# A softmax attention and feed-forward kernel whose on-chip tiles get new start addresses

## The chip, the cores and the metric

The kernel runs on one core of one Trainium2 chip. The metric is the device time of one execution in microseconds; below, a time of the kernel is the median of several runs.

## What is computed

All tensors are float32. The reference, cut to what matters:

```python
S, D, F, H, Dh = 2048, 512, 1792, 32, 16
xn = layernorm(x)                                # over D, eps 1e-5
q, k, v = split_heads(xn @ wqkv)                 # 32 heads of 16
s = merge_heads(softmax(q @ k.T * Dh ** -0.5) @ v) @ wo
h = maximum(xn @ w1 + b1, 0) ** 2                # the squared ReLU
out = x + s * silu(h @ w2 + b2)
```

## The kernel before

Everything runs in one program whose order of instructions is written out by hand (`tc.manual_schedule()`); the tile framework adds only the waits between engines. `fast_path` does all the work. `general_path` follows it in a branch that is not taken here.

**Precision.** Most products take float32 operands split in a rounded high part (type float32r, suffix `h` in tile names) and a rest (suffix `l`), and add three products: high with high, high with low, low with high. Values and row sums use plain float32.

**Stage one**, some 150 us. Four chunks of 512 rows are normalised and transposed into `xT` (tiles KA0 and KA1 for chunks 0 and 2, and xh0, xh1, xl0, xl1 for chunks 1 and 3). `linear` (line 117) makes the values: for each block of 128 rows, 12 products of 128 rows by 128 columns against 512 columns of the weights, which lie split in wf1h0, P8, wf1l0 and P9. Queries and keys are made by a Strassen-Winograd scheme from products of half blocks: `product` (line 305) adds six products of 128 x 128 against 512. Its weights (the stationary side) lie in wf2, hh, hl, or, as sums, in KA2, P6 and P7 and other P tiles; its right sides (the moving side) in KA0 and KA1, xh and xl, or, for sums, in u, y, P14, P15, V0, V1. The results go to DRAM and come back later, permuted.

**Stage two**, 64 turns of about 16.5 us. A turn covers 8 blocks of 128 keys for four heads and 512 queries. For each block, `score` (line 494) makes four products on half the rows, two at a time on rows 0 to 63 and 64 to 127: the weights are 128 keys of KA0, KA1 or KA2 (which take turns, in this order, with every load of 1,024 keys), the right side is QA0 or QA1. ScalarE takes the exponentials (line 498) into the tiles P0 to P15, a pair for each of eight blocks; VectorE copies a part of the scores out first (line 517). Between the score products, in an order given by a string of letters, stand products of the feed-forward layers (line 542), also on half the rows in pairs: `first` (weights wf1h0 and wf1l0, right sides xh and xl) and `second` (weights hh and hl, right sides wf2h and wf2l). In the middle of a turn `swap` changes the banks of the two halves, with a memset of one element on GpSimd as a fence (line 568). At the end of the turn the values of the eight blocks follow as one row (line 841): 64 records of TensorE, four heads on four groups of 32 columns, with weights from V0 or V1 (16 key blocks of 83 words each, `NK` and `QW` in the code) and right sides from P.

**The last turns** multiply by the output weights and add the gate and x.

**Addresses.** A tile is named by its tag. The pool `keep` lies first in a partition, then the pool `sb`. In each pool a tag gets its place at its first request, behind the tags that were asked for before, its size rounded up to 32 bytes a partition; later tiles of the tag use the same place. `keep` begins 128 bytes behind a multiple of 512, with `ident` (512 bytes a partition), `nvalid` (4) and `stat` (320). In `sb` the order is that of the code's first use: `ou0`, `b1t`, `eps`, `b2b`, `note`, `P4`, `KA2`, `P5`, `QA0`, `QA1` and so on, with tiles of a few bytes (`st0`, `rs0`, `mv0`, `okm`) among the large ones.

```python
return (p or ps.get(tag, sb)).tile(shape, dt, tag=tag, name=f"{tag}_{cnt[0]}")
```

Of the kernel before, what the change touches and what calls it, by code (L numbers as in the profile page):

```python
# [24 lines left out]
FT = mybir.dt.float32  # L25
FR = mybir.dt.float32r
I32 = mybir.dt.int32
# [11 lines left out]
NK = S // 128  # L39
VW = 560  # L40
QW = 83
# [6 lines left out]
@with_exitstack  # L48
def mha_ffn_kernel(ctx: ExitStack, tc: tile.TileContext, x, wqkv, wo, bx, w1, b1, w2, b2, out):
    nc = tc.nc  # L50
    x, out = x[0], out[0]
    ctx.enter_context(tc.manual_schedule())
    keep = ctx.enter_context(tc.tile_pool(name="keep", bufs=1))
    dram = ctx.enter_context(tc.tile_pool(name="dram", bufs=1, space=DRAM))

    ident = keep.tile([128, 128], FT, name="ident")
    make_identity(nc, ident)
    nvalid = keep.tile([1, 1], I32, name="nvalid")
    stat = keep.tile([128, 80], FT, name="stat")

    kdram = [[dram.tile([128, 2, 1024], FT, name=f"kd{g}_{h}") for h in range(2)] for g in range(4)]
    qdram = [[dram.tile([128, 2, 512], FT, name=f"qd{g}_{c}") for c in range(NC)] for g in range(4)]
    vdram = dram.tile([NK, 128, VW], FT, name="vd")
    xdram = [dram.tile([128, 2, 4, 512], FT, name=f"xd{c}") for c in range(3)]
    sdram = {(a, p): dram.tile([128, 2, 4, 2, 128], FT, name=f"sd{a}{p}") for a in "kq" for p in range(2)}

    udram = [[dram.tile([2, 2, 16, 4, 512], FT, name=f"ud{g}_{c}") for c in range(NC)] for g in range(4)]
    zdram = [[dram.tile([4, 512], FT, name=f"zd{q}_{c}") for c in range(NC)] for q in range(NQ)]
    gdram = dram.tile([S, D], FT, name="gd")

    with tc.tile_pool(name="sb", bufs=1) as sb, ExitStack() as banks:
        fast_path(tc, sb, banks, locals())
    general_path(tc, dram, nvalid, ident, vdram, kdram, qdram, gdram, x, wo, out)


def fast_path(tc, sb, banks, env):
    nc = tc.nc
    ident, nvalid, stat = (env[n] for n in ("ident", "nvalid", "stat"))
    kdram, qdram, vdram, xdram, sdram, udram, zdram, gdram = (
        env[n] for n in ("kdram", "qdram", "vdram", "xdram", "sdram", "udram", "zdram", "gdram"))  # L80
    x, wqkv, wo, w1, b1, w2, b2, out = (
# [9 lines left out]
    def t(shape, dt, tag):  # L91

        cnt[0] += 1
        if tag in BUFS:
            turn[tag] = turn.get(tag, -1) + 1
            n = turn[tag] % BUFS[tag]
            p, tag = ps.get(tag), f"{tag}{places[n] if tag == 'S' else n}"
        else:
            p = None
        return (p or ps.get(tag, sb)).tile(shape, dt, tag=tag, name=f"{tag}_{cnt[0]}")  # L100

    def cast(eng, dst, src):
        if eng is act:
            act.copy(dst, src)
        else:
            eng.tensor_copy(dst, src)  # L106
# [16 lines left out]


    b1raw = t([14, 128], FT, "ou0")
    b1t = t([128, 14], FT, "b1t")
    eps = t([128, 1], FT, "eps")
    dve.memset(eps, EPS)
    b2b = t([128, D], FT, "b2b")

# [423 lines left out]
    note, notes = t([1, 128], FT, "note"), [0]  # L554
# [264 lines left out]
    tags = (("P2", "gl", "P1"), ("P3", "P6", "P7"), ("wf2h0", "wf2l0", "wf2h1"), ("wf2l1", "gl", "KA2"))  # L819
# [196 lines left out]
    for j, c in enumerate(ORDER):  # L1016
        for i in range(2):
            n = per * (j + 1) + i - 1 if j < 3 else LAST + 2 + i
# [85 lines left out]
    for n in range(TURNS):  # L1104
        i = 8 * n
# [68 lines left out]
    ok, okm, ones = t([128, 80], FT, "ok"), t([128, 1], FT, "okm"), t([128, 1], FT, "ones")  # L1174
# [162 lines left out]
```

## Time and profile before

| | |
|---|---|
| Time, median of 3 runs | 1218.28 us (1217.95 to 1218.51) |
| Time of the profiled execution | 1218.33 us |
| Its span, first to last instruction | 1216.6 us |
| Mean granted clock of TensorE | 0.998 |
| TensorE products, busy | 1205.6 us, 99%, 9877 instructions |
| ScalarE, busy | 1042.8 us, 86% |
| VectorE, busy | 846.7 us, 70% |
| GpSimd, busy | 350.4 us, 29% |

How to read the profile's lines. PE is TensorE (PEld its weight loads), ACT is ScalarE, DVE is VectorE, POOL is GpSimd; L117 is line 117 of the kernel. A line of the page's first part gives busy time, share of the span and number of instructions of each engine; the chain of work that ended last tells whose work filled the span. A line of the waits reads: who waited, for whom, us in total, how often, the longest. A line of the timeline gives the start in us, the length in us, engine, line and operation, tile written and tiles read, then the sizes and the number of instructions that follow one another (x2); the end of a product is modelled, and products overlap, so the rate of products is read from the distance of the starts. A line of the table by stretches gives the stretch, its length and the busy time (with the number of instructions) of the engines, then the granted clock, the busy share of the DMA engines and the GB/s; where it is asked for one line of the kernel, only TensorE's products and weight loads appear.

### The profile page before, as it was taken

What the parts mean: (1) busy time and instruction counts of PE and PEld (TensorE: products, weight loads), DVE (VectorE), ACT (ScalarE), POOL (GpSimd) and SP (SyncE); (2) the same over time, 40 slices, a digit from 0 to 9 for tenths busy, and PEclk for the clock granted to TensorE, in tenths of its full rate; (3) what the DMA queues carried; (4) which work ended last, traced back from release to release, by engine and by line L of the source; (5) the groups of instructions that cost most, each with busy time, mean ns of one, the idle gap of its engine ahead of it and who ended that gap; (6) DMA issues with size and microseconds to landing.
All of it is one profiled execution on the core that took longest, in us unless ns stands there. A gap on an engine that the chain in (4) does not pass through costs nothing.

```text
span 1216.6 us, 24228 instructions
## 1 busy us (share of the span) xinstructions
PE 1205.6 (99%) x9877; PEld 714.0 (59%) x9877; DVE 846.7 (70%) x1365; ACT 1042.8 (86%) x1231; POOL 350.4 (29%) x268
## 2 busy tenths in 40 slices
PE   9999999999999999999999999999999999999996
PEld 8888755555555555555555555555555555655553
DVE  7666777576767776757677666667775758777776
ACT  6645589899889889888999888889898889999983
POOL 5756523040312320304032122221230403222222
PEclk9999999999999999999999999999999999999999
DMA  7799915131353223224423133151422232465544
GB/s 289 279 357 317 358 58 136 42 112 45 96 153 91 83 65 81 79 79 148 119 75 99 60 89 93 45 169 48 126 79 80 77 99 80 131 198 159 156 136 106
DMA packets 107576, 154.91 MB, mean 127 GB/s; under 512 B 43386, under 2 KB 57736, under 8 KB 107460
## 3 DMA queue, kind: packets, MB, share of 16 engines
q1 hardware_dynamic: 104804, 144.93, 37.7%
q0 software_dynamic: 2368, 7.87, 2.2%
q8 instruction: 78, 1.28, 0.4%
q10 hardware_dynamic: 288, 0.52, 0.1%
q14 instruction: 38, 0.31, 0.1%
HBM read 103.61 MB, written 49.67 MB: 126 GB/s over the span
## 4 chain that ended last, share of the span: by engine, by line
PE 96%; DVE 1%; POOL 1%; DMA 1%; issue 0%; SPq 0%; ACT 0%; DVEq 0%; POOLq 0%
PE acc L841 36%; PE S L542 28%; PE S L494 14%; PE acc L494 5%; PE B L305 5%; PE B L117 3%; PE lin L494 2%; PE D L305 1%; PE B L672 1%; DMA hl<-gd 1%; PE D L243 0%; PE S L984 0%; PE lin L305 0%; PE acc L305 0%; SPq L871 0%
## 5 line engine op out<-in xcount | busy, mean ns | idle before, releaser
L498 ACT ACTIVATE P<-S 128x1024 f32<-128x1024 f32 x702 | 662.8, 1035 | 94.3 <-PE S L494 92.4
L841 PE MATMUL acc<-P,V 128*32 128x512 f32 x4096 | 453.6, 594 | 0.0
L517 DVE COPY P<-acc 128x512 f32<-128x512 f32 x322 | 222.6, 691 | 140.0 <-PE lin L494 67.3
L498 ACT ACTIVATE P<-P 128x1024 f32<-128x1024 f32 x322 | 314.5, 1082 | 0.0
L841 PEld LDWEIGHTS acc<-P,V 128*32 128x32 f32 x4096 | 126.1, 110 | 287.0 <-issue 265.5
L494 PE MATMUL S<-QA,KA 64*128 64x512 f32 x1404 | 291.7, 403 | 0.0
L517 DVE COPY P<-lin 128x512 f32<-128x512 f32 x322 | 220.4, 684 | 2.7 <-PE lin L494 0.6
L494 PEld LDWEIGHTS S<-QA,KA 64*128 64x128 f32 x1404 | 135.3, 184 | 108.2 <-issue 41.8
L494 PE MATMUL lin<-QA,KA 64*128 64x512 f32 x322 | 127.6, 396 | 0.0
L494 PE MATMUL acc<-QA,KA 64*128 64x512 f32 x322 | 127.1, 395 | 0.0
L110 POOL TENSOR_TENSOR wf1l<-wr,wf1h 128x1024 fp32r<-128x1024 f32 x28 | 68.5, 2446 | 176.6 <-DVE wf1h L106 108.3
L568 POOL MEMSET note<- 1x1 f32 x68 | 6.0, 88 | 385.2 <-PE S L542 383.7
L542 PE MATMUL S<-xl,wf1h 64*128 64x512 f32 x464 | 96.5, 390 | 0.0
L110 POOL TENSOR_TENSOR hl<-T,hh 128x1024 fp32r<-128x1024 f32 x28 | 80.1, 2861 | 52.9 <-DVE hh L106 52.9
L110 POOL TENSOR_TENSOR wf2l<-wr,wf2h 128x1024 fp32r<-128x1024 f32 x28 | 67.7, 2417 | 90.3 <-DVE wf2h L106 90.3
L542 PE MATMUL S<-xh,wf1l 64*128 64x512 f32 x480 | 91.7, 391 | 0.0
L542 PE MATMUL S<-wf2l,hh 64*128 64x512 f32 x448 | 91.3, 390 | 0.0
L867 DVE TENSOR_TENSOR ou<-acc,ou 128x512 f32<-128x512 f32 x31 | 21.4, 692 | 96.6 <-PE acc L841 86.8
L542 PE MATMUL S<-wf2h,hl 64*128 64x512 f32 x448 | 83.8, 390 | 0.0
L542 PE MATMUL S<-xh,wf1h 64*128 64x512 f32 x480 | 77.9, 392 | 0.0
L542 PE MATMUL S<-wf2h,hh 64*128 64x512 f32 x448 | 72.3, 394 | 0.0
L494 PEld LDWEIGHTS acc<-QA,KA 64*128 64x128 f32 x322 | 59.3, 184 | 16.5 <-DVE P L517 2.4
(370 smaller groups left out, 1432.2 us busy)
## 6 DMA issues: line engine op xcount, KB each, us to landing
wr<-in_B_w_dram SPq DMA_DIRECT2D x56, 512.0 KB
QA<-qd SPq DMA_DIRECT2D x128, 128.0 KB
KA<-kd SPq DMA_DIRECT2D x64, 256.0 KB
u<-ud SPq DMA_DIRECT2D x15, 512.0 KB
kd<-P SPq DMA_DIRECT2D x11, 512.0 KB
V<-vd SPq DMA_DIRECT2D x8, 664.0 KB
qd<-P SPq DMA_DIRECT2D x9, 512.0 KB
vd<-P SPq DMA_DIRECT2D x16, 280.0 KB
```

Of the source, the lines that this page charges most:

```text
L110: leng.tensor_tensor(lo, src, hi.bitcast(FT), op=OP.subtract)
L117: mm(dst, lhs(a, k), rhs(b, k), start=n == 0, stop=n == len(todo) - 1)
L305: mm(dst, left[a][:, k], right[b][:, k], start=n == 0, stop=n == 5)
L494: mm(dst, k[r, p, 128 * (kb % 8):128 * (kb % 8) + 128], q[r, p], start=True, stop=True)
L498: act.activation(ptile[i, p], src, AF.Exp, scale=SCALE)
L517: dve.tensor_copy(ptile[i, p][:, hp], sides[hp])
L542: ins = mm(bank, self.lhs(a, k)[r], self.rhs(b, k)[r], start=n == 0 and self.at[other] == 0, stop=n == len(self.todo[half]) - 1 and self.a ...
L568: f = pool.memset(note[:, notes[0]:notes[0] + 1], 0.0)
L672: mm(idle[:, :128], ident, ident, start=True, stop=True)
L841: mm(sides[0][32 * j:32 * j + 32], vq[qd][:, kb, 17 * j:17 * j + 32], ptile[i, j // 2][:, j % 2], start=first, stop=last)
L867: dve.tensor_tensor(ou, sides[0], part[0], op=OP.add)
```

## The change

No instruction is added, taken away or moved. In `keep`, the three small tiles (`eps` is now one of them) are asked for ahead of `ident`. At the head of `fast_path`, every large tag of `sb` is asked for once, at its full size, in a new order: the sixteen P tiles, the KA tiles, the QA and split tiles, the others of the same size, then the smaller ones, and between V0 and V1 (5,312 bytes each) small tiles that fill up to the next multiple of 512. These first tiles are never read or written; they only fix the places. `ident` and all large tiles then begin at a multiple of 512 bytes. The slices that TensorE reads inside a tile begin 512 bytes apart or a multiple of it, but for those of V, which begin 332 bytes apart from key block to key block and 68 from head to head, as before.

```diff
+    nvalid = keep.tile([1, 1], I32, name="nvalid")
+    stat = keep.tile([128, 80], FT, name="stat")
+    eps = keep.tile([128, 1], FT, name="eps")
     ident = keep.tile([128, 128], FT, name="ident")
     make_identity(nc, ident)
-    nvalid = keep.tile([1, 1], I32, name="nvalid")
-    stat = keep.tile([128, 80], FT, name="stat")
...
+    split_tiles = [f"{a}{n}" for a in ("xh", "xl", "wf2h", "wf2l", "hh", "hl") for n in range(2)]
+    for tags, n in (((f"P{i}" for i in range(16)), 1024), (("KA0", "KA1", "KA2"), 2048),
+                    (("QA0", "QA1", "wf1h0", "wf1l0", *split_tiles), 1024),
+                    (("T0", "T1", "wr0", "wr1", "gl", "u0", "u1", "y0", "y1"), 1024), (("ou0", "ou1", "b2b"), 512),
+                    (("note",), 128), (("V0",), NK * QW), (("st0", "st1"), 12), (("rs0", "rs1", "mv0", "mv1"), 8),
+                    (("okm", "warm"), 1), (("V1",), NK * QW)):
+        for tag in tags:
+            sb.tile([128, n], FT, tag=tag, name=f"{tag}_first")
...
-    eps = t([128, 1], FT, "eps")
     dve.memset(eps, EPS)
```

More of the change, by code (lines that the diff above doesn't have):

```diff
@@ L77, in fast_path @@
     nc = tc.nc
-    ident, nvalid, stat = (env[n] for n in ("ident", "nvalid", "stat"))
+    ident, nvalid, stat, eps = (env[n] for n in ("ident", "nvalid", "stat", "eps"))
     kdram, qdram, vdram, xdram, sdram, udram, zdram, gdram = (
```

## The prediction

> **What bounds the kernel now.** I read the page first, then the waits, then the order of TensorE's own instructions.
>
> ```profile
> span 1216.6 us, 24228 instructions
> PE 1205.6 (99%) x9877; PEld 714.0 (59%) x9877; DVE 846.7 (70%) x1365; ACT 1042.8 (86%) x1231; POOL 350.4 (29%) x268
> ...
> PE 96%; DVE 1%; POOL 1%; DMA 1%; issue 0%; SPq 0%; ACT 0%; DVEq 0%; POOLq 0%
> ```
>
> The span is 1216.6 us and the profiled execution took 1218.33 us, so 1.7 us lie around the span; the median of the runs is 1218.28. Sums below go against 1218.3. TensorE is busy for 99% and makes 96% of the chain that ended last. A layout changes no instruction, so it must change the time of TensorE's steps, or of what TensorE waits for.
>
> ```profile
> ACT P L498 <- PE S L494: 92.4, 73, 2.4
> ...
> PEld S L494 <- ACT P L498: 18.6, 88, 0.8
> ```
>
> In the view of waits ScalarE waits 92.4 us for TensorE's scores. TensorE's weight loads wait 18.6 us for ScalarE, part of it under running products. So a TensorE that is some 10 us faster finds the room it needs, and one that is slower puts the whole loss on the span.
>
> **The rate of products against the start addresses.** The pool lays its tags in the order in which they are first asked for, each rounded up to 32 bytes, so the starts of the kernel before, taken modulo 512 bytes, come out as these: KA0, KA1, wf1h0, wf1l0, P8, P9 at 352; KA2, QA0, QA1, P4 to P7, P10 to P12 at 64; wf2, hh, hl, V0, T1 at 32; x, u, y, P0 to P3, P13 to P15 at 224. Slices of a tile (V's apart) start 512 bytes or a multiple of that further on, so a product keeps the remainders of its two tiles. The same product of line 117, with the same right sides (wf1, P8, P9 at 352), runs twice:
>
> ```profile
> 62.29 0.63 PE L117 MATMUL B<-P,KA 128*128 128x512 f32 x2
> 62.76 0.62 PE L117 MATMUL B<-wf1l,KA 128*128 128x512 f32 x2
> 63.22 0.62 PE L117 MATMUL B<-P,KA 128*128 128x512 f32 x2
> 63.67 0.61 PE L117 MATMUL B<-wf1h,KA 128*128 128x512 f32 x2
> ...
> 72.75 0.62 PE L305 MATMUL D<-xh,KA 128*128 128x512 f32 x2
> ```
>
> ```profile
> 99.78 0.62 PE L117 MATMUL B<-wf1h,xh 128*128 128x512 f32 x2
> ...
> 110.94 0.40 PE L305 MATMUL D<-xh,KA 128*128 128x512 f32 x1
> ```
>
> With weights from KA0 and KA1 (352, the remainder of the right side) the 40 products from 63.67 to 72.75 us take 9.08 us, 227 ns each; the pieces of two start every 0.45 or 0.46 us throughout. With weights from xh and xl (224 against 352) the 48 products from 99.78 to 110.94 take 11.16 us, 232.5 ns each. The run with equal remainders does not start at its rate: the pieces at 62.29 and 62.76 are 0.47 and 0.46 us before the next, about 233 ns a product, and only then does it settle.
>
> ```profile
> 62.00:73.00 11.00, 11.00 (x50) 9.05 (x50) 5.91 (x13) 5.55 (x9) 6.20 (x4) 1.00 0.99 314
> 99.50:111.00 11.50, 11.50 (x51) 9.31 (x51) 10.15 (x15) 6.43 (x13) 5.74 (x5) 1.00 0.85 296
> ```
>
> The faster stretch has the busier DMA (0.99 against 0.85) and the same clock (1.00), so neither makes the difference. VectorE is less busy in it (5.91 of 11.00 us against 10.15 of 11.50), which a third and a fourth row weigh:
>
> ```profile
> 47.46 1.57 PE L305 MATMUL B<-u,KA 128*128 128x512 f32 x6
> 48.87 1.57 PE L305 MATMUL B<-y,KA 128*128 128x512 f32 x6
> ```
>
> ```profile
> 22.55 0.62 PE L305 MATMUL B<-KA,wf2l 128*128 128x512 f32 x2
> 23.00 1.08 PE L305 MATMUL B<-KA,wf2h 128*128 128x512 f32 x4
> 23.92 0.62 PE L305 MATMUL B<-KA,wf2l 128*128 128x512 f32 x2
> 24.38 1.08 PE L305 MATMUL B<-KA,wf2h 128*128 128x512 f32 x4
> 25.29 0.62 PE L305 MATMUL B<-KA,wf2l 128*128 128x512 f32 x2
> 25.75 1.18 PE L305 MATMUL B<-KA,wf2h 128*128 128x512 f32 x4
> ```
>
> ```profile
> 46.00:51.70 5.70, 5.70 (x26) 4.55 (x26) 2.79 (x13) 2.42 (x6) 5.70 (x6) 1.00 0.30 112
> 22.00:27.50 5.50, 5.50 (x26) 4.32 (x25) 5.34 (x15) 4.36 (x7) 3.82 (x4) 1.00 1.04 403
> ```
>
> Weights from KA2 (64) against u (224): six products in 1.41 us, 235 ns each, with VectorE at 2.79 of 5.70 us and DMA at 0.30. Weights from wf2 (32) against KA0 (352): 14 products in 3.20 us, 228.6 ns, with VectorE at 5.34 of 5.50 and DMA at 1.04. So the step follows the two addresses and not the company: 227 ns for equal remainders, 228.6 for 32 against 352, 232.5 for 224 against 352, 235 for 64 against 224. Each pairing repeats whenever it comes back.
>
> [...]
>
> **The change, part by part.**
>
> *Stage one* (up to 150 us, products over all 128 rows):
>
> ```profile
> 0.00:150.00 150.00, 45.87 (x192) 35.51 (x192) 1.00 0.90 324
> ```
>
> ```profile
> 0.00:150.00 150.00, 80.87 (x336) 62.40 (x336) 1.00 0.90 324
> ```
>
> ```profile
> 40.40 0.70 PE L117 MATMUL B<-wf1h,xh 128*128 128x512 f32 x2 [0.18 <-ACT y L337]
> ```
>
> The rows are line 117 (192 products) and line 305 (336). By the code, half of the 192 (chunks 0 and 2, weights from KA) are of the 227 ns kind and the other 96 of the 232.5 kind; of the 336, the 16 products of six with KA on the right, 96, are of the 228.6 kind, and the other 240 near 235. After the change all pairings are 0 against 0. If they run as 352 against 352 do: 96 x 5.5 + 96 x 1.6 + 240 x 8 ns = 2.6 us. A quarter of these products lies ahead of 40.40 us, where TensorE waits for ScalarE and VectorE's chain anyway, so I take 2.0 us; bounds 0 and 2.6.
>
> *The scores and the feed-forward products* (lines 494 and 542) run as pairs on the two halves of the rows, 40 pairs in a turn (16 of scores, 24 of the other), 64 turns:
>
> ```profile
> 150.00:1200.00 1050.00, 434.18 (x2012) 225.81 (x2012) 1.00 0.33 99
> 150.00:1200.00 1050.00, 502.01 (x2988) 321.66 (x2988) 1.00 0.33 99
> ```
>
> ```profile
> 621.00 0.62 PE L542 MATMUL S<-xh,wf1h 64*128 64x512 f32 x4
> ...
> 629.81 0.40 PE L494 MATMUL S<-QA,KA 64*128 64x512 f32 x2
> ```
>
> 5,000 products (2012 of line 494 and 2988 of 542) are 2,500 pairs; in the turn shown the 38 steps from 621.00 to 629.81 take 8.81 us, 232 ns a pair. Here scores (KA at 352 or 64 against QA at 64) alternate with feed-forward pairs (352 against 224, or 32 against 32), so no long row of equal remainders ever occurs, and what it would do is not in the trace. The lower bound is the settled 227 ns: 5 ns x 38 x 64 = 12.2 us. The other bound is no gain. What the trace has on partly equal turns:
>
> ```profile
> 266.28 7.00 PE acc L841 x64
> 282.83 7.00 PE acc L841 x64
> 299.31 7.00 PE acc L841 x64
> 315.82 7.00 PE acc L841 x64
> ```
>
> Between the values (7.00 us) the section takes 9.55, 9.48 and 9.51 us. The first and third have their scores from KA2 (64, as QA), the second from KA0 (352). The first has equal remainders inside each kind, scores and feed-forward both, and is not faster. So equality of one product is not enough; the row at 62 us says why it need not be, since there too the first six products cost 231 ns. A turn of the changed kernel has two runs of about 19 steps between its start, the swap's fence and the values. Six at 231 and 13 at 227 make 228, 4 ns less than 232: 38 x 64 x 4 ns = 9.7 us. That pairs on half the rows settle as full products do is an inference, so I take somewhat less, 8 us.
>
> *The values* (line 841): V is read in slices of 83 words per key block, 332 bytes apart, which stay off the 512-byte grid. P's tiles at 64, 224 and 352 already give the same 7.00 us in every turn above. Nothing is taken or added, and 0 is used.
>
> *The rest.* The extra tiles that the change asks for are never written, so no instruction, wait or DMA comes with them; eps keeps its memset. Transfers keep their number and sizes. DMA at 0.99 above lies beside a TensorE busy 11.00 of 11.00 us, so a faster or slower transfer is covered; uncovered it would show first in the opening microseconds. [...]
>
> Sum: 1218.3 - 2.0 - 8.0 = 1208.3 us.
>
> **Rivals.**
> *The half-row pairs don't settle.* For it: the 9.55 us turn; the two halves of a pair are issued one after the other and may keep disturbing each other. Against: every full-row pairing has its own steady rate. Then only stage one gains, 0.5 to 2.6 us: 1215.7 to 1217.8, about 1216.8.
> *Weights that start at a multiple of 64 are the slow ones.* The row at 235 ns has its weights in KA2, at 64, and both turns with KA2 are slower than the one with KA0. The rows cannot part "unequal remainders" from "weights on a multiple of 64", as the row of KA2 is unequal too. After the change all weights except V's start on such a multiple. At 235 ns each, pairs lose 3 ns x 38 x 64 = 7.3 us and stage one 96 x 8 + 96 x 2.5 + 96 x 6.4 ns = 1.6 us: 1227, which I take. If pairs lose as KA2's turns do, 0.03 to 0.07 us for 16 of the 40 pairs, it is 0.08 to 0.17 us a turn, 5 to 11 us in all, and with stage one 1225 to 1229. It decides as soon as a pair costs over 1 ns more than the 232 of now.
> *The address doesn't act at all* (the rates above come from which tiles are written at the time): 1218.3. Against it: 227 and 235 ns stand beside a VectorE that is about half busy each time. [...]
>
> **How the numbers follow.** Forecast 0.58, pairs that don't settle 0.20, slow multiples of 64 0.17, no action 0.05. The forecast's own range runs from 1203.5 (all 12.2 and 2.6 us) to 1215. The range takes in the second and fourth cases and, below, 2 us for steps at fences that the sum left alone: 1201.5 to 1219. What is left out is the slow case. About 0.2%, 2.4 us, is what a measurement of this kernel can tell from no change. Faster by more: 0.58 and a fifth of the second case, 0.62. Slower by more: 0.17. Within: 0.21.
>
> **What would show it.** Right: pieces of line 117 every 0.45 us in both stretches, at 62 and at 100 us; line 305's six products in 1.36 us instead of 1.41; the sections between values at 9.3 to 9.4 us instead of 9.5, the values still 7.00, and ScalarE's wait for scores below 92.4 us. Wrong: line 117 fast but the sections still at 9.5 (second case), or six products of line 305 still in 1.41 us and sections of 9.55 and above (third). A wait of TensorE for VectorE or ScalarE in place of the gain would show in the waits of the weight loads.

## The result, and the profile after

| | before | after |
|---|---|---|
| Time, median (lowest to highest) | 1218.13 us (1217.59 to 1219.80), 6 runs | 1213.33 us (1212.48 to 1214.04), 6 runs |
| Time of the profiled execution | 1218.33 us | 1212.94 us |
| Its span | 1216.6 us | 1211.2 us |

The ratio after to before is 0.9958, with a 95% interval of 0.9945 to 0.9971: faster by 4.8 us, where 10 were forecast. Below, lines of the new kernel stand 9 or 10 higher than before (L117 is now L127, L305 L314, L494 L503, L498 L507, L517 L526, L542 L551, L841 L850).

The page after, its first lines and two lines of the waits (who waited, for whom, us in total, times, the longest):

```profile
span 1211.2 us, 24228 instructions
...
PE 1200.1 (99%) x9877; PEld 709.9 (59%) x9877; DVE 845.4 (70%) x1365; ACT 1040.8 (86%) x1231; POOL 350.1 (29%) x268
```

```profile
ACT P L507 <- PE S L503: 91.9, 73, 2.3
...
PEld S L503 <- ACT P L507: 22.7, 105, 0.8
```

The numbers of instructions are the same and TensorE is still busy for 99%. Two lines already hint at what follows: ScalarE's wait for scores has hardly shrunk (92.4 to 91.9 us), and TensorE's weight loads now wait for ScalarE 105 times where it was 88 (22.7 us, before 18.6).

Stage one in the timeline (start, length, instruction); the rate is read from the distances of the starts:

```profile
62.62 0.62 PE L127 MATMUL B<-P,KA 128*128 128x512 f32 x2
63.08 0.62 PE L127 MATMUL B<-wf1h,KA 128*128 128x512 f32 x2
63.53 0.62 PE L127 MATMUL B<-P,KA 128*128 128x512 f32 x2
...
98.61 0.61 PE L127 MATMUL B<-wf1l,xh 128*128 128x512 f32 x2
99.07 0.62 PE L127 MATMUL B<-P,xh 128*128 128x512 f32 x2
99.52 0.62 PE L127 MATMUL B<-wf1h,xl 128*128 128x512 f32 x2
...
108.59 0.62 PE L314 MATMUL D<-xh,KA 128*128 128x512 f32 x2
```

```profile
46.30 1.52 PE L314 MATMUL B<-u,KA 128*128 128x512 f32 x6
47.66 1.52 PE L314 MATMUL B<-y,KA 128*128 128x512 f32 x6
```

Both stretches of line 127 now have a piece of two every 0.45 us: the 44 products from 98.61 to 108.59 us take 226.8 ns each, where the same weights from xh and xl took 232.5. Six products of line 314 take 1.36 us instead of 1.41. Before and after, the first values and four later ones in the chain:

```profile
149.98 7.00 PE acc L841 x64
```

```profile
147.04 7.00 PE acc L850 x64
...
262.97 7.00 PE acc L850 x64
279.43 7.00 PE acc L850 x64
295.90 7.00 PE acc L850 x64
312.35 7.00 PE acc L850 x64
```

The values keep their 7.00 us; the sections between them take 9.46, 9.47 and 9.45 us, where it was 9.55, 9.48 and 9.51. Over all turns of the ordinary order (52 before, 53 after) the mean section is 9.504 us before and 9.466 after.

Where the span's 5.4 us are: 0.8 before the first product of line 127, which starts at 8.90 us before and 8.09 after; 2.1 from there to the first values (149.91 and 146.97 by their own records); 2.55 in the sections (600.84 to 598.28 us in all); nothing in the values (448.82 in both); 0.1 is lost behind the last turn. The 0.8 is no gain of the layout. A later kernel with the changed layout and an unchanged stage one started that product at 9.27 us. The three rows, of before, after and that kernel:

```profile
8.90 1.73 PE L117 MATMUL B<-wf1h,KA 128*128 128x512 f32 x6
```

```profile
8.09 2.02 PE L127 MATMUL B<-wf1h,KA 128*128 128x512 f32 x6
```

```profile
9.27 1.74 PE L127 MATMUL B<-wf1h,KA 128*128 128x512 f32 x6
```

So stage one gave the 2 us of the forecast, and the loop gave 2.55 us where 8 were forecast. Why the loop gave so little is what most of the experiments are about.

### The profile page after: what moved, and what is told of

It is laid out like the page before. It is cut to its first block, busy times and chain, and to the rows that moved or that the text cites. A ratio compares the mean times of both kernels' runs of the same rounds, so it can differ in the third digit from the quotient of the medians.

```text
span 1211.2 us, 24228 instructions
## 1 busy us (share of the span) xinstructions
PE 1200.1 (99%) x9877; PEld 709.9 (59%) x9877; DVE 845.4 (70%) x1365; ACT 1040.8 (86%) x1231; POOL 350.1 (29%) x268
## 4 chain that ended last, share of the span: by engine, by line
PE 97%; DVE 1%; DMA 1%; SPq 0%; issue 0%; ACT 0%; DVEq 0%
PE acc L850 36%; PE S L551 28%; PE S L503 14%; PE B L314 5%; PE acc L503 5%; PE B L127 4%; PE lin L503 2%; PE D L314 1%; PE D L252 1%; DMA hl<-gd 0%; PE S L993 0%; PE lin L314 0%; SPq L880 0%; PE acc L314 0%; DMA P<-in_A_x_dram 0%
## 5 line engine op out<-in xcount | busy, mean ns | idle before, releaser
L507 ACT ACTIVATE P<-S 128x1024 f32<-128x1024 f32 x702 | 661.9, 1040 | 93.7 <-PE S L503 91.9
L850 PE MATMUL acc<-P,V 128*32 128x512 f32 x4096 | 453.6, 594 | 0.0
L526 DVE COPY P<-acc 128x512 f32<-128x512 f32 x322 | 222.8, 692 | 139.7 <-PE lin L503 69.2
L507 ACT ACTIVATE P<-P 128x1024 f32<-128x1024 f32 x322 | 315.0, 1090 | 0.0
L850 PEld LDWEIGHTS acc<-P,V 128*32 128x32 f32 x4096 | 126.3, 110 | 285.6 <-issue 265.6
L503 PE MATMUL S<-QA,KA 64*128 64x512 f32 x1404 | 292.0, 405 | 0.0
L526 DVE COPY P<-lin 128x512 f32<-128x512 f32 x322 | 220.6, 685 | 1.5 <-PE lin L503 0.6
L503 PEld LDWEIGHTS S<-QA,KA 64*128 64x128 f32 x1404 | 134.6, 184 | 111.2 <-issue 41.8
L503 PE MATMUL lin<-QA,KA 64*128 64x512 f32 x322 | 126.8, 394 | 0.0
L503 PE MATMUL acc<-QA,KA 64*128 64x512 f32 x322 | 126.6, 393 | 0.1
L551 PE MATMUL S<-xl,wf1h 64*128 64x512 f32 x464 | 95.8, 389 | 0.0
L551 PE MATMUL S<-xh,wf1l 64*128 64x512 f32 x480 | 91.3, 388 | 0.0
L551 PE MATMUL S<-wf2l,hh 64*128 64x512 f32 x448 | 90.3, 390 | 0.0
L551 PE MATMUL S<-wf2h,hl 64*128 64x512 f32 x448 | 82.9, 388 | 0.0
L551 PE MATMUL S<-xh,wf1h 64*128 64x512 f32 x480 | 77.7, 392 | 0.0
L551 PE MATMUL S<-wf2h,hh 64*128 64x512 f32 x448 | 71.7, 393 | 0.0
L503 PEld LDWEIGHTS acc<-QA,KA 64*128 64x128 f32 x322 | 59.3, 184 | 17.1 <-DVE P L526 2.4
```

What stands on the lines that cost most here:

```text
L503: mm(dst, k[r, p, 128 * (kb % 8):128 * (kb % 8) + 128], q[r, p], start=True, stop=True)
L507: act.activation(ptile[i, p], src, AF.Exp, scale=SCALE)
L526: dve.tensor_copy(ptile[i, p][:, hp], sides[hp])
L551: ins = mm(bank, self.lhs(a, k)[r], self.rhs(b, k)[r], start=n == 0 and self.at[other] == 0, stop=n == len(self.todo[half]) - 1 and self.a ...
L850: mm(sides[0][32 * j:32 * j + 32], vq[qd][:, kb, 17 * j:17 * j + 32], ptile[i, j // 2][:, j % 2], start=first, stop=last)
```

## The experiments

### What the address does to one product, by itself

A program that runs only rows of 40 products on rows of x: the weights of a row start at one remainder modulo 512, the right sides at another, as the name says (f32w0r: weights at 32, right side at 0; h for pairs on the two halves of the rows, o for one half alone).

> Only rows of products: on rows of x, 24 rows of 40 products 128x128 against 512, 16 rows of 40 pairs on the two halves of the rows, and 3 rows of 40 products on one half alone, each row with its own two remainders modulo 512 bytes of the weights' and the right side's start. Nothing of the reference is computed. Theory one (equal remainders are what counts): rows with 0 and 0, 32 and 32, 64 and 64, 352 and 352 all settle at 227 ns a product, rows with unequal ones at 229 to 235 ns, whichever side is moved. Rival two (the weights' place on a grid of its own counts, the right side's does not): rows with weights at one remainder agree, whatever the right side. Rival three (the address does not act, the company does): all rows alike. For pairs on half rows: the forecast's theory has the equal rows at 227 ns a step after some six steps, with the second half's product a fixed time behind the first; its rival has them at 232 throughout.

The timeline of TensorE, start and length of each row:

```profile
36.75 9.24 PE L54 MATMUL f0w0r<-r,w 128*128 128x512 f32 x40
45.83 9.26 PE L54 MATMUL f32w32r<-r,w 128*128 128x512 f32 x40
...
73.12 9.48 PE L54 MATMUL f32w0r<-r,w 128*128 128x512 f32 x40
82.44 9.49 PE L54 MATMUL f64w0r<-r,w 128*128 128x512 f32 x40
91.77 9.53 PE L54 MATMUL f96w0r<-r,w 128*128 128x512 f32 x40
101.14 9.46 PE L54 MATMUL f128w0r<-r,w 128*128 128x512 f32 x40
...
119.78 9.33 PE L54 MATMUL f192w0r<-r,w 128*128 128x512 f32 x40
128.95 9.49 PE L54 MATMUL f224w0r<-r,w 128*128 128x512 f32 x40
138.27 9.23 PE L54 MATMUL f256w0r<-r,w 128*128 128x512 f32 x40
147.34 9.49 PE L54 MATMUL f320w0r<-r,w 128*128 128x512 f32 x40
```

```profile
267.79 9.28 PE L61 MATMUL h32w32r<-r,w 64*128 64x512 f32 x80
276.89 9.29 PE L61 MATMUL h352w352r<-r,w 64*128 64x512 f32 x80
285.99 9.51 PE L61 MATMUL h32w0r<-r,w 64*128 64x512 f32 x80
```

From the start of f0w0r to the next row are 9.08 us, 227 ns a product; f32w0r takes 9.32, f96w0r 9.37, f192w0r 9.17, and f256w0r is back at 9.07. Read product by product, the last 24 distances of each row have these means:

| weights' start less right side's, modulo 256 | distance, full rows | distance, pairs on half rows |
|---|---|---|
| 0 (0/0, 32/32, 352/352, 256/0, 0/256) | 226.7 ns | 226.7 ns |
| 192 (192/0, 448/0, 32/352) | 228.9 | 228.9 |
| 128 (128/0, 384/0, 224/352) | 232.1 to 232.8 | 232.1 to 232.8 |
| 32, 64, 160, 224 | 233.3 | 233.3 (32 and 64; the other two were not run) |
| 96 (96/0, 64/224) | 234.3 to 234.4 | 234.3 to 234.5 |

Each product is as far from the next as the difference of the two starts modulo 256 bytes says, wherever either lies: theory one, with a smaller period than the 512 bytes of the new layout. The rivals (weights on a grid of their own, the company) fall. A row reaches its own rate whatever the rate of the row ahead of it, but some rows need eight products or so to find it (f32w32r: 230, 224, 231, 235, 229, 232, 231, 227, then 226 to 228); f256w0r, behind a row at 233, has its 227 ns from the first product. Pairs on half rows settle exactly as full products do, so the rival of the prediction by which they don't falls too. Two rows stand outside the table: 0 against 64 on half rows stayed at 233.3 where the same addresses on full rows gave 228.9, and 0 against 384 on full rows at 233.3 where others with 128 gave 232 to 233. There can be more than one steady pattern for a pairing.

226.7 and 234.4 ns, with VectorE, ScalarE and GpSimd idle, show that the two starts together set the distance of the products. Why they do, no run here shows.

### Equal remainders that are not zero

```diff
+    sb.tile([128, 8], FT, tag="pad", name="pad_first")
     split_tiles = [...]
```

> The changed kernel with a small tile of 32 bytes ahead of the list, so that every large tile of the loop starts 32 bytes behind a multiple of 512; the remainders stay equal among themselves. Theory one (equal remainders): no change against the changed kernel, 1213.3 us, sections between values 9.47 us, pieces of line 127 every 0.45 us. Rival (multiples of 512, or of 64, are what helps): back towards the time before, 1216 to 1218 us.

1213.87 us, ratio 0.9966 (0.9953 to 0.9979), as the changed kernel; the 39 steps of a turn (the distances of its 40 pairs) take 9.127 us against 9.128. So no grid of 512, nor one of 64, is needed, and the rival of slow multiples of 64 is gone from the other side as well. The run answers one more rival: that transfers gain from tiles that start at multiples of 512. With the shift no large tile of the loop starts there, and the time stays.

### Right sides 160 and 256 bytes off

```diff
-                    (("QA0", "QA1", "wf1h0", "wf1l0", *split_tiles), 1024),
+                    (("wf1h0", "wf1l0", "hh0", "hh1", "hl0", "hl1"), 1024),
                     (("T0", ..., "y1"), 1024), (("ou0", "ou1", "b2b"), 512),
+                    (("off",), 40), (("QA0", "QA1", *split_tiles[:8]), 1024),
```

(40 words are 160 bytes; the second kernel has 64 words, 256 bytes.)

> The changed kernel with the loop's right sides (QA0, QA1, xh, xl, wf2h, wf2l, and V0, V1, the notes) 160 bytes behind a multiple of 512, and the weights (KA, wf1, hh, hl) and P left on it. In stage one a part of the pairings becomes unequal as well (weights from xh, xl and wf2, right sides V0 and V1), worth up to 1.5 us of the 2.9. Theory one (equal remainders): the loop falls back to 232 ns a step, sections between values 9.50 us instead of 9.47, step at the swap 238 instead of 269; 1215 to 1218 us. Rival (the weights' place counts): sections stay at 9.47, 1213.3 to 1214.8.

> The same as the run with the right sides 160 bytes off, but with 256 bytes: QA0, QA1, xh, xl, wf2h, wf2l, V0, V1 start 256 bytes behind a multiple of 512, the weights on it. Theory (what counts is the difference of the two starts modulo 256, as in the rows of products by themselves, where 256 against 0 settles at 226.7 ns): no change against the changed kernel, sections 9.47 us, 1213.3. Rival (modulo 512): slower, as with 160 bytes, sections 9.56 us, 1220.

Values in the chain, with 160 bytes first, then with 256:

```profile
266.41 7.00 PE acc L851 x64
282.96 7.00 PE acc L851 x64
299.52 7.00 PE acc L851 x64
```

```profile
279.43 7.00 PE acc L851 x64
295.91 7.00 PE acc L851 x64
312.34 7.00 PE acc L851 x64
```

With 160 bytes: sections of 9.55 and 9.56 us, 1220.41 us, ratio 1.0022 (1.0012 to 1.0031), slower than before, and by more than was expected. Its steps are 234 ns, as the rows by themselves: weights at 0 less right sides at 160 is 96 modulo 256, and the table has 234.4 for 96. The kernel before had a mixture of equal and unequal pairs, at 232. With 256 bytes: sections of 9.48 and 9.43 us, 1212.57 us, ratio 0.9957 (0.9940 to 0.9974), the changed kernel's time. The loop obeys the table.

### The stop at the swap: VectorE's copy?

Read pair by pair over 51 turns, the mean steps are these (in ns; step 0 is the distance from pair 0 of a turn to pair 1, and so on; a step is the mean of both halves; the last three columns belong to experiments further down, the last two to the later pair with short exponentials):

| steps of a turn | before | after | 160 off | new order | short exps, after | short exps, before |
|---|---|---|---|---|---|---|
| 1 to 10 | 232.1 | 231.4 | 233.8 | 231.8 | 231.6 | 232.2 |
| 11 to 18 | 232.0 | 227.0 | 234.1 | 228.9 | 227.5 | 231.9 |
| 19, behind the swap | 238.3 | 269.2 | 232.3 | 229.6 | 231.6 | 232.0 |
| 20 to 29 | 233.5 | 232.3 | 234.6 | 232.7 | 232.8 | 233.4 |
| 30 to 38 | 231.8 | 229.9 | 233.9 | 226.7 | 227.4 | 231.6 |
| all 39 (step 0 is 337 to 338), us | 9.175 | 9.128 | 9.232 | 9.083 | 9.080 | 9.165 |

The changed kernel settles at 227 from step 11 on, stops at step 19 for some 37 ns more, and then does not settle again until the end. My first theory was VectorE: pair 20, the second behind the swap, needs the side bank `lin`, and starts 1.39 us after the single product 1 that filled it, where six steps of 227 ns are 1.36. (I took the 1.39 us for the time until VectorE's copy out of the bank ends. That copy ends 1.12 us behind the product, so the trace spoke against the theory before the run.)

```diff
-    ORDINARY = "SLLSBLLLSLL0SL1LSLL/SBLLSLL0SL1LSLL0L1SLS"
+    ORDINARY = "SLLSBLLLSLL0S1LLSLL/SBLLSLL0SL1LSLL0L1SLS"
```

(The order of the first turn gets the same move.)

> The changed kernel with one letter of the order moved: the side bank's single product 1 in the first half of a turn comes one step earlier, so that seven steps and not six lie between it and the product behind the swap that needs that bank again. Theory (a new wait): that product waits for VectorE's copy out of the bank, a fixed 1.39 us, which six steps of 232 ns covered and six of 227 don't. Then the step of 269 ns at the swap falls to about 235 (31 ns x 52 turns = 1.6 us), and if the stop is also what sends the products back to 231 ns, the second half of the turn gains up to 4 ns x 18 steps more: 1208 to 1211.7 us in all, against 1213.3. Rival (the fence of the swap itself, a memset of GpSimd, costs the 31 ns): no change, 1213.3.

1213.68 us, ratio 0.9963 (0.9949 to 0.9976), and step 19 at 270.1 ns. The theory falls: VectorE's copy now ended 0.38 us before that pair instead of 0.28, and the pair was as late as ever. The rival of this run, the fence, was not shown by it either. What keeps its distance in both kernels is ScalarE: pair 20 starts 389 ns behind the end of ScalarE's fourth exponential of the turn, with a spread of 2 ns after and 1 ns with the letter moved (before, 393 with a spread of 5). The timeline of the changed kernel around one swap: the fourth score pair of the turn, then TensorE's products at the swap, its weight load there, ScalarE's fourth exponential, then its nine exponentials as one row:

```profile
569.95 0.40 PE L503 MATMUL S<-QA,KA 64*128 64x512 f32 x2
...
571.08 0.63 PE L551 MATMUL S<-wf2h,hl 64*128 64x512 f32 x4
571.53 0.44 PE L503 MATMUL S<-QA,KA 64*128 64x512 f32 x2
571.81 0.39 PE L503 MATMUL acc<-QA,KA 64*128 64x512 f32 x1
```

```profile
571.47 0.19 PEld L503 LDWEIGHTS S<-QA,KA 64*128 64x128 f32 x2 [0.19 <-ACT P L507]
```

```profile
570.40 1.02 ACT L507 ACTIVATE P<-S 128x1024 f32<-128x1024 f32 x1
```

```profile
567.64 8.36 ACT L507 ACTIVATE P<-S 128x1024 f32<-128x1024 f32 x9 [1.55 <-PE S L503]
```

The weight load of the score pair at 571.53 waits 0.19 us for ScalarE: a score pair needs the bank of the pair before the last, and its exponential must have read it. I read the last row so: from 567.64 us on ScalarE runs nine exponentials back to back, 0.93 us each, so that score pairs four steps of 227 ns apart (0.91 us) run into it. The next runs call this ScalarE's pace.

Read one by one, the exponentials say something else about why. The sixth to ninth, which find their scores ready, start 0.904 us after one another, in both kernels. The third to fifth start 0.43 us behind the second product of their own score pair, so ScalarE waits for TensorE there; its records (1.02 us each) overlap, so that no gap shows. What TensorE runs into is the round trip of one bank. From the fourth score pair (569.95) to its exponential (570.40) are 0.45 us, the exponential takes 1.02, and from its end to pair 20 (571.81) are 0.39: 1.86 us in the mean of the changed kernel, 1.87 in the one before. TensorE has eight steps for it, 1.86 us at 232 ns and 1.81 at 227. So before, the steps nearly covered the round trip, and after the change TensorE comes some 45 ns too early.

### ScalarE's pace: later score pairs

```diff
-    ORDINARY = "SLLSBLLLSLL0SL1LSLL/SBLLSLL0SL1LSLL0L1SLS"
+    ORDINARY = "SLLSBLLLSL0LS1LLSLL/BSLLLSL0LS1LLSL0L1SLS"
```

> The changed kernel with the letters of a turn in another order: the score pairs 6 to 9 (steps 19, 23, 27, 31) come one step later each, behind B at the swap, and the single products 0 and 1 of the first half one step earlier; no instruction is added. The run with 1 moved alone showed the stop at the swap unchanged at 270 ns, so VectorE's copy is not its cause. New theory (ScalarE's pace): a score pair needs the bank of the pair before the last, which ScalarE empties at 0.94 us a pair, back to back from the turn's start; pairs four steps of 227 ns apart (0.91 us) catch up with it. One step later each, nobody waits: the stop at the swap falls from 269 to 227 to 240 ns, the second half goes from 231.2 towards 228 ns a step, 50 to 90 ns a turn, 51 turns, 2.6 to 4.6 us: 1208.7 to 1210.7. Rival (it is the change of banks at the swap, or the mix of score and feed-forward pairs, that keeps the products from settling): 1213.3 within 0.7.

> The same new order of letters on the kernel before. Theory (ScalarE's pace): at 232 ns a step the score pairs hardly meet ScalarE (step at the swap 238 ns, 6 over the others), so it gains 0 to 0.5 us: 1217.2 to 1217.7. Rival (the new order is better by itself, whatever the addresses): as much as on the changed kernel, 3 us or more.

On the changed kernel 1212.39 us (1211.85 to 1212.82), ratio 0.9951 (0.9938 to 0.9965); on the kernel before 1217.58 us, ratio 0.9998 (0.9989 to 1.0007), as expected. On the changed kernel the steps do what both readings of ScalarE say, since TensorE now has nine steps for a bank's round trip: 229.6 at the swap, 226.7 from step 30 on, 45 ns less for the 39 steps. The time, expected at 1208.7 to 1210.7, does not follow: the mean section went from 9.466 to 9.445 us only. The end of the same turn in this kernel, ScalarE's row and TensorE's last score pair and first values:

```profile
568.60 8.42 ACT L507 ACTIVATE P<-S 128x1024 f32<-128x1024 f32 x9 [1.42 <-PE S L503]
```

```profile
577.13 0.44 PE L503 MATMUL S<-QA,KA 64*128 64x512 f32 x2
577.50 1.06 PE L850 MATMUL acc<-P,V 128*32 128x512 f32 x8
```

ScalarE's ninth exponential ends at 577.02 and the values start 0.48 us later; in most turns of this kernel that distance is 476 to 484 ns, never under 476, while it was 532 on average in the changed kernel and 552 in the one before. The last score pair waits for that exponential. It is a round trip again, now with seven steps for it: from the ninth score pair to the values are 1.95 us, and 1.96 in the kernel before with the same order. So of TensorE's gain of 45 ns some 20 came back as a wait at the end of the turn, and the turn now ends as early as that round trip lets it. This version is ahead of both kernels by its median and its sections; against the changed kernel the intervals of the two ratios overlap, so its 0.9 us are not settled.

### ScalarE out of the way

If the wait for ScalarE is the limit, by its pace or by the round trip, shorter exponentials must let the addresses do more. In four kernels the exponentials that read the score banks take 416 of 512 columns, and GpSimd fills the rest with ones, first right behind each exponential, then in one row behind the fence and one at the turn's end.

```diff
-            act.activation(ptile[i, p], src, AF.Exp, scale=SCALE)
+            n = 512 if src is ptile[i, p] else 416
+            act.activation(ptile[i, p][:, :, :n], src[:, :, :n], AF.Exp, scale=SCALE)
+            if n < 512:
+                pool.memset(ptile[i, p][:, :, n:], 1.0)
```

> The changed kernel with ScalarE's load made smaller: the exponentials of the score pairs that go straight from their bank take 416 of each 512 columns, and GpSimd fills the other 96 with ones; the output is not the reference's. It takes some 0.15 us from each of 704 instructions of ScalarE and leaves TensorE's order and addresses as they are. Theory (ScalarE's pace): no score pair waits for its bank, the step at the swap falls to about 230, the products stay settled at 227 ns through the second half: 0.10 to 0.14 us a turn, 51 turns, 5 to 7 us: 1206 to 1208. Rival (the mix or the swap keeps them from settling): 1213.3 within 1 us.

> The kernel before with the same shorter exponentials (416 of 512 columns, ones from GpSimd in the rest; not the reference's output). Both theories: TensorE's steps stay at 232 ns, the step at the swap falls from 238 to 233; 1217 to 1217.6. Against the changed kernel with the same exponentials it shows what the addresses are worth where ScalarE is out of the way: theory one 9 to 11 us, its rival about 5.

1218.40 us on the changed kernel, 1225.38 on the one before: both times are far above what was expected, as the fills stood ahead of the fence on GpSimd. The weight loads' wait for the fence in the first of the two:

```profile
PEld S L554 <- POOL note L580: 16.6, 54, 1.2
```

In the changed kernel that wait is 2.0 us. The steps agree with the theory (232.8 at the swap, 226.6 at the end of the turn), the times can't speak for it. Hence the second pair of kernels, where `fill_tails` writes the ones that `tails` has collected (the edit is against the first pair):

```diff
-                pool.memset(ptile[i, p][:, :, n:], 1.0)
+                tails.append(ptile[i, p][:, :, n:])
...
                 swap()
+                fill_tails()
...
+        fill_tails()
         for a in later:
             exps(*a)
```

> The changed kernel with the exponentials of 416 of 512 columns again, but GpSimd's fills now stand in one row behind the fence of the swap and one at the end of the turn, so that the fence no longer waits behind them. The output is not the reference's. Theory (ScalarE's pace): no stop at the swap (230 to 235 ns), settled steps of 227 in both halves, the 39 steps of a turn 9.03 to 9.07 us instead of 9.13, sections 9.37 to 9.42 us; 1207.5 to 1210 if the fills hide. Rival (mix or swap): sections stay at 9.46.

> The kernel before with the same shorter exponentials and late fills (not the reference's output). Theory: steps stay at 232 ns, sections 9.48 to 9.50 us, 1216.5 to 1218. The difference to the changed kernel with the same exponentials is what the addresses are worth with ScalarE out of the way: 0.09 to 0.13 us a turn, with stage one 7 to 10 us in all. Rival (mix or swap): difference of 5 us as between the two originals.

1209.50 us on the changed kernel (ratio 0.9930, 0.9914 to 0.9947) and 1216.95 on the one before (0.9991, 0.9982 to 1.0001). On the changed kernel the shorter exponentials take 864 ns each, where the full ones took 1040. Values in the chain, the changed kernel first:

```profile
263.48 7.00 PE acc L859 x64
279.88 7.00 PE acc L859 x64
296.30 7.00 PE acc L859 x64
```

```profile
265.34 7.00 PE acc L850 x64
281.87 7.00 PE acc L850 x64
298.37 7.00 PE acc L850 x64
```

Sections of 9.40 and 9.42 us against 9.53 and 9.50; on average 9.405 and 9.494, a difference of 89 ns a turn where the originals differ by 39. The addresses are worth 7.4 us with the shorter exponentials and 4.8 with the full ones. The stop at the swap is gone (231.6 ns), and the last steps of the turn run at 227; the 39 steps take 9.080 us, a little more than the 9.03 to 9.07 expected. That the wait for ScalarE's exponentials cost the loop some 50 ns a turn is shown. These runs don't part ScalarE's pace from the round trip, as a shorter exponential shortens both; for the round trip speak the starts of the exponentials.

One more stop is left. Step 21 takes 245 ns in the kernel before, 258 in the new order and 250 with the shorter exponentials on the changed kernel. In every turn the weight load there waits 0.15 to 0.18 us for the fence of the swap, GpSimd's memset. In the changed kernel, whose TensorE has just stopped for ScalarE, the step takes 233. It is a part of the row of steps 20 to 29 in the table; what it is worth was not tried.

## Why the prediction was right, and where it was not

**The address.** The forecast's mechanism held: equal starts run at 227 ns, full rows and half rows alike, and the prices read from four pairings of the trace (227, 228.6, 232.5, 235) are those of the rows by themselves (226.7, 228.9, 232 to 233, 234.3). It was worded too narrowly: starts that differ by 256 bytes are as good as equal ones. The time alone would not show this: 1213.33 us lies between the forecast's 1208.3 and the 1216.8 of the pairs that don't settle, nearer to the second, and the range was drawn wide enough for both. The rows of products and the runs with moved tiles show it.

**Stage one.** 2.0 us forecast, 2.1 measured behind the opening (141.0 to 138.9 us from the first product of line 127 to the first values). In the kernel with the moved letter, where stage one is the same, it was 1.65. The term stands.

**The pairs.** This is the term that was mis-sized: 8.0 us forecast, 2.55 measured. It fell short in two ways. The first is the settling. The prediction took 231 ns for the first six steps and 227 for the rest, 228 in the mean, 4 less than before. In the new order, without the stop, both halves of a turn have 230, 2 less than before: some ten steps, not six, run at 231 to 233 behind the values and behind the swap. That fits the 89 ns a turn with the shorter exponentials, some 5 us of the 8.

**The step that failed** is the second: the sentence that ScalarE's 92.4 us of waiting are room for a TensorE some 10 us faster. It put any new wait of TensorE for ScalarE at nothing. The row of before that contradicts it is this, ScalarE in one turn, with TensorE's first products of that turn:

```profile
571.16 0.50 PE L494 MATMUL S<-QA,KA 64*128 64x512 f32 x2
```

```profile
571.70 8.40 ACT L498 ACTIVATE P<-S 128x1024 f32<-128x1024 f32 x9 [1.53 <-PE S L494]
```

Nearly all of ScalarE's waiting in the turn is one piece of 1.53 us ahead of the first exponential, two thirds of it while the values run. It is no room for the steps inside the turn. There a score pair waits for the exponential that empties its bank, and the round trip of 1.86 us stays what it is when TensorE's eight steps shrink from 1.86 to 1.81. So of the forecast's 0.125 us a turn (8 us in 64 turns) some 0.05 went into waits for ScalarE, by the 89 ns with short exponentials against 39 with full ones; the new order got 20 ns of that back. ScalarE's load alone would have left the room: eight starts 0.904 us apart and a last exponential of 1.03 us are an estimate of 8.26 us for the nine that take 8.40 in the row. In the trace the exponentials that read P start 0.947 us apart, and those that read a score bank 0.904 where they need not wait.

**What would have shown it.** Of the signs named, line 117 in both stretches, line 305's 1.36 us and the values' 7.00 came as forecast. The sections (9.46 instead of 9.3 to 9.4) did not, and the last sign, a wait of TensorE for ScalarE in place of the gain, came: 105 waits instead of 88 in the weight loads' row.

**The rivals.** Pairs that don't settle, and slow multiples of 64, are refuted by the rows of products and by the shift of 32 bytes; in the kernel the pairs do settle, only later than was taken. That the address doesn't act is refuted by the 160 bytes, which cost 7 us against the changed kernel with nothing else altered but places. The upper time of the slow case, 1229 us, is a slip of the sum: with stage one's 1.6 us its 11 us give 1231. Nothing else hangs on it.

**What stays open.** Why the opening before the first product of line 127 differs by over 1 us between executions (8.09 to 9.27 us) was not tried; it moves single spans by as much as a quarter of the gain. Nor is it known what has the period of 256 bytes, or why the first ten steps of a turn don't settle sooner; before and after, a weight load waits some 0.13 us for VectorE at the fifth pair of each turn, which was not tried either.

## What to carry to other kernels

Where an engine looks busy for 99%, look at the order of its partner inside one turn before counting the partner's idle time as room: 92 us of waiting in one piece per turn is no slack for the steps in the turn. Add up the round trip of each bank that the two hand to and fro, and compare it with the steps between its two uses: here 1.86 us against eight steps of 227 ns. Where products of TensorE, 128x128 against 512 columns as here, follow each other with new weights each time, let the two operands start at addresses that are equal modulo 256 bytes; it is worth up to 3% of such a row (226.7 against 234.4 ns), costs no instruction (24228 before and after), and rows by themselves show it in one run. A faster engine may need a new order: the same order that did nothing for the kernel before (0.9998) took the stop away after the change, though the time that it gained there, 0.9 us, is not settled.

## What the runs showed of the hardware that was not expected

In the rows by themselves the distance of two 128x128 products against 512 columns went by the difference of their operands' starts modulo 256: 226.7 ns at 0, 228.9 at 192, 232 to 233 at 128, 233.3 at 32, 64, 160 and 224, 234.4 at 96, at a granted clock of at least 0.9 in every slice of 11 us from 30 to 400 us of that program (0.988 in the mean of all of it). After a stop or a change of pairing a row can need eight to ten products to reach its rate, so a short wait can cost a second time: with the shorter exponentials on the changed kernel the steps behind the 250 ns of step 21 run at 229 to 233 until step 28, and at 227 only from step 32 on.

ScalarE's exponentials of 1,024 columns that have work waiting start 0.904 us apart when they read a score bank and 0.947 when they read P. Their records overlap, so a row of them without a gap can still hide waits: the third to fifth of each turn start 0.43 us behind their score pair, 0.93 us apart before and 0.92 after.
